# Sixteen modulation columns of an adaLN block: from VectorE reductions to TensorE column groups, with the first loads in another order

## The chip, the cores and the metric

The kernel runs on one core of one Trainium2 chip. The metric is the device time of one execution in microseconds (us). A core has five engines with a queue of instructions each: TensorE (PE in the profile, its weight loads PEld), VectorE (DVE), ScalarE (ACT), GpSimd (POOL) and SyncE (SP), which here issues the DMAs. Each engine works through its own queue in order; semaphores tie the queues together.

## The reference, cut to what matters

```
mod = (silu(c) @ w_mod).reshape(1, 6, 1, 1024)
sa, ca, ga, sb, cb, gb = (mod[:, i] for i in range(6))
h = layernorm(x) * (1 + ca) + sa
x = x + ga * attention(h, wq, wk, wv, wo, beta)
h = layernorm(x) * (1 + cb) + sb
out = x + gb * ((gelu(h @ w_gate) * (h @ w_up)) @ w_down)
```

The input x has 2048 rows of 1024. The attention works on 4 segments of 512 rows with 32 heads of 32, and carries a memory matrix from segment to segment. `c` is one row of 1024 and `w_mod` is 1024 by 6144, so `mod` is one row of 6144 numbers: 48 columns of 128 in the kernel's layout. The first 16 columns are sa (0 to 7) and ca (8 to 15). The very first product of the attention needs them.

## The kernel before, in words

The kernel has three parts: a startup, the attention (32 steps, one for each half of the segments, group of four heads and segment), and the feed-forward, which takes some two thirds of the time.

In the startup, segment 0 of x (four tiles of 128 rows, each in two halves `x0`) is normalised: `norm_seg_stats` takes mean and variance on VectorE (`bn_stats` L233, `bn_aggr` L236, add L238), raises to the power -1/2 on GpSimd (L239), forms the shift on VectorE (`mr`, L244) and scales on ScalarE (L246). `norm_seg` then makes, for each of the 8 slices kt of 128 model columns, four transposes on TensorE (`tpa`, L330), one ScalarE pass that applies the modulation (`h`, L332: column kt of `modT` as the shift, column 8 + kt as the scale), a rounded copy on ScalarE (`hha`, L335) and the remainder on VectorE (`hla`, L336). Products of two fp32 numbers are made of three with such pairs. `first_part` is the first use: for each kt it multiplies `hha` and `hla` with the k, v and q weights of group 0 (12 products of 256 columns at L366, three of 512 at L372), which are themselves split in pairs by `split_w` (L197 on ScalarE, L199 on VectorE).

A modulation column comes from `mod_col` (L188): 128 rows of `w_mod` transposed, 1024 long, are multiplied with `scb` (silu(c), repeated on all 128 partitions) and summed on VectorE; a scale column gets 1.0 added (L193). `scb` is made by `row_of` through two products on TensorE (L162) and two copies on ScalarE (L163). The 16 first columns take 16 loads of 512 KB into 8 buffers (`wm_a` to `wm_d`, two halves each), in the order scale, shift for kt = 0, 1, and so on. The other 32 columns are made the same way, one or two in each later step.

The order of TensorE's and SyncE's instructions in the startup is the program's. On VectorE, ScalarE and GpSimd a planner orders them by the program's order and by when it expects the inputs; only an instruction under `keep_in_program_order` is pinned behind the instruction that the program gave to its engine just before. That holds for the `bn_stats` of segment 1 (`norm_stats`, L229 to L235). The startup's loop (L1432) runs

```
for kt, _ in enumerate(first_part(0, 0, 0)):
    next(nseg, None)
    if kt == 1:
        W[0][2] = split_w(raw0[1], wsp_tile("w0_1"), nc.vector)
    if kt >= 4:
        norm_seg_stats(1, x1h, (kt - 4,))
```

With two turns of `norm_seg` taken ahead of it, the order is: products of kt, transposes of kt + 2, and from kt = 4 on the statistics of one tile of segment 1. Step 0 then opens with the eight turns of `norm_seg(1, ...)`, the transposes of segment 1 (first tile to last), followed by its k and v products. The loads are issued as: c, beta, 8 of x0 (256 KB each), the weights k, v and q of group 0 (512 KB each), 8 columns of `w_mod`, 8 more as buffers come free, and 4 of segment 1 (512 KB each).

Two copies on ScalarE (L1439) fill 32 partitions of the two key tiles `ks` (2048 elements each) with a constant pattern `selj`.

Of the kernel before, what the change touches and what calls it, by code (L numbers as in the profile page):

```python
# [14 lines left out]
ALU = mybir.AluOpType  # L15
# [4 lines left out]
P = 128  # L20
# [13 lines left out]


@with_exitstack
def block_kernel(ctx: ExitStack, tc: tile.TileContext, x, c, wmod, wq, wkv, wo, beta, wg, wu, wd, out):
    nc = tc.nc
    f32 = lambda ap: ap.bitcast(F32)

# [29 lines left out]
    def tmp_tile(name):  # L70
        return big.tile([P, L], F32, name=name, tag="tmp", bufs=4)
# [8 lines left out]
    def s_ps(name):  # L80
        return psum.tile([P, L], F32, name=name, tag="s", bufs=5)
# [4 lines left out]
    def t2(name, tag, bufs=1, dt=F32, shape=(P, L)):  # L86
        return (p1 if tag in ("qs", "row") else pa).tile(list(shape), dt, name=name, tag=tag, bufs=bufs)

    def cs(shape, name, dt=F32, **kw):
        return const.tile(shape, dt, name=name, **kw)  # L90
# [1 line left out]

    ccol = cs([P, KT], "ccol")
    nc.sync.dma_start(ccol, c)
    bb = cs([P, H], "bb")
    nc.sync.dma_start(bb, bass.AP(tensor=beta.tensor, offset=beta.offset, ap=[[0, P], [1, H]]))
    def fetch(src, name):
        r = raw_tile("r" + name)
        nc.sync.dma_start(r, src)
        return r  # L100

    x0 = [[], []]
    for i in range(4):
        for h in range(2):
# [1 line left out]
            t = t2(f"x0_{i}_{h}", tag, bufs=bufs)  # L106
            nc.sync.dma_start(t, x[i * P:(i + 1) * P, h * L:(h + 1) * L])
            x0[h].append(t)
    raw0 = [fetch(wkv[0, 0], "k0"), fetch(wkv[0, 1], "v0"), fetch(wq[0], "q0")]


    ones = cs([P, P], "ones")
# [33 lines left out]
    def sigmoid(dst, src):  # L146
        nc.scalar.activation(dst, src, AF.Exp, scale=-1.0)
        nc.vector.tensor_scalar_add(dst, dst, 1.0)
        nc.vector.reciprocal(dst, dst)
# [16 lines left out]
    def row_of(*a):  # L166
        for _ in row_parts(*a):
            pass
# [1 line left out]
    scol = cs([P, KT], "scol")  # L170
    sigmoid(scol, ccol)
    nc.vector.tensor_mul(scol, scol, ccol)
    scb = t2("scb", "row", shape=(P, D))
    row_of(scb, scol, tmp_tile, "sc")
    gall = cs([P, H], "gall")
    sigmoid(gall, bb)
    omg = pa.tile([P, H], F32, name="omg")
    nc.vector.tensor_scalar(omg, gall, -1.0, 1.0, op0=ALU.mult, op1=ALU.add)
    modT = cs([P, 48], "modT")

    def mod_load(r, w=None):
        if w is None:
            w = raw_tile(f"wm{r}")
        nc.sync.dma_start(w, wmod[r])
        return r, w

    def mod_col(r, w, behind=False):
        i = nc.vector.tensor_tensor_reduce(out=w, in0=w, in1=scb, scale=1.0, scalar=0.0,  # L188
                                           op0=ALU.mult, op1=ALU.add, accum_out=modT[:, r:r + 1])
        if behind:  # L190
            tc.keep_in_program_order(i)
        if r // 8 in (1, 4):
            nc.vector.tensor_scalar_add(modT[:, r:r + 1], modT[:, r:r + 1], 1.0)  # L193
# [256 lines left out]
    def first_part(n, g, s):  # L450

        nm = f"{g}_{s}"
        kn, vx = kv_tiles(n, nm)
        kv = [(mm_ps if t < 2 else s_ps)(f"kv{nm}_{t}") for t in range(4)]
        psq = o_ps("q" + nm)
        for kt in range(KT):
            for t in range(4):
                kv_mm(kv[t][:, :2 * P], g, s, t, kt)
            q_mm(psq, g, s, kt)
            yield  # L460
        for t in range(4):
            kv_out(kv[t][:, :2 * P], kn, vx, t, 1)
        k_out(n, s, nm, kn, vx)
        q_out(n, s, nm, psq)
# [947 lines left out]
    with tc.manual_schedule(engines={mybir.EngineType.PE}):  # L1412
        with tc.manual_schedule(engines={mybir.EngineType.SP}):
            free = [wsp_tile("wm_a"), wsp_tile("wm_b")] + [
                t2(f"wm_{q}", "qs", bufs=2, dt=F32R, shape=(P, 4, L)).rearrange("p (a b) t -> p a (b t)", a=2) for q in "cd"]
            spare = [f32(w[:, h]) for w in free for h in range(2)]
            order = [r for kt in range(KT) for r in (8 + kt, kt)]
            got = [mod_load(r, spare[i]) for i, r in enumerate(order[:8])]
            norm_seg_stats(0, x0)
            W[0] = [None] * 3  # L1420
            for i in (0, 2):
                W[0][(1, 2, 0)[i]] = split_w(raw0[i], wsp_tile(f"w0_{i}"), nc.vector)
            nseg = norm_seg(0, x0)
            for i, r in enumerate(order):
                mod_col(*got[i])
                if i + 8 < len(order):
                    got.append(mod_load(order[i + 8], spare[i % 8]))
                if i in (1, 3):
                    next(nseg)
            x1h = [fetch(x[L + i * P:L + (i + 1) * P, :], f"x1_{i}") for i in range(4)]  # L1430
            x1h = [[t[:, h * L:(h + 1) * L] for t in x1h] for h in range(2)]
            for kt, _ in enumerate(first_part(0, 0, 0)):  # L1432
                next(nseg, None)
                if kt == 1:
                    W[0][2] = split_w(raw0[1], wsp_tile("w0_1"), nc.vector)
                if kt >= 4:
                    norm_seg_stats(1, x1h, (kt - 4,))
        for k in ks_t:
            nc.scalar.activation(k[96:128], selj[96:128].unsqueeze(2).to_broadcast([32, 4, L]), AF.Copy)  # L1439
        norm_a = norm_tiles(x, hT_d, (2, 3), 1, 0, "a")  # L1440
        next(norm_a)
        for n in range(len(steps) + 1):
            work = {k: none for k in "VSAMKQN"}
            if n > 0:
                work["V"] = values(n - 1, *steps[n - 1][1:])
            if n < len(steps):
                work["S"] = scores(n, *steps[n][1:])
                work["A"] = sums(n, *steps[n][1:])
                work["M"] = memory(n, *steps[n][1:])
            work["N"] = norm_seg(1, x1h) if n == 0 else norm_a  # L1450
            side = none
            if n in (14, 15):
                hT[n - 12] = []
                side = load_hT(hT_d, n - 12, hT[n - 12], f"h{n - 12}")
            if n == 30:
                side = load_hT(oT_d, 0, oh[0], "o0")
            if n + 1 < len(steps):
                _, g, s = steps[n + 1]
                work["K"] = kv_part(n + 1, g, s)
                work["Q"] = q_part(n + 1, g, s)  # L1460
            else:
# [81 lines left out]
```

## Time and profile before

| | |
|---|---|
| time, median of 3 runs | 2927.32 us |
| lowest and highest run | 2924.64, 2929.8 us |
| the profiled execution, its own time | 2932.13 us |
| span of its trace | 2930.4 us |
| TensorE busy | 2838.5 us, 97% of the span |
| TensorE busy in the first 73 us (first of 40 slices) | five tenths; 9 tenths in nearly all others |
| VectorE, ScalarE, GpSimd busy | 64%, 43%, 30% |
| granted TensorE clock, mean | 0.992 |

The busy shares are averages over stages with different limits. The span begins with the first instruction of the trace; all times in the rows below count from there.

### The profile page before, as it was taken

What the parts mean: (1) busy time and instruction counts of PE and PEld (TensorE: products, weight loads), DVE (VectorE), ACT (ScalarE), POOL (GpSimd) and SP (SyncE); (2) the same over time, 40 slices, a digit from 0 to 9 for tenths busy, and PEclk for the clock granted to TensorE, in tenths of its full rate; (3) what the DMA queues carried; (4) which work ended last, traced back from release to release, by engine and by line L of the source; (5) the groups of instructions that cost most, each with busy time, mean ns of one, the idle gap of its engine ahead of it and who ended that gap; (6) DMA issues with size and microseconds to landing.
All of it is one profiled execution on the core that took longest, in us unless ns stands there. A gap on an engine that the chain in (4) does not pass through costs nothing.

```text
span 2930.4 us, 48825 instructions
## 1 busy us (share of the span) xinstructions
PE 2838.5 (97%) x17248; PEld 2534.1 (86%) x17248; DVE 1860.8 (64%) x4293; ACT 1265.3 (43%) x3112; POOL 882.6 (30%) x1428
## 2 busy tenths in 40 slices
PE   5999999999999999999999999999999999999998
PEld 4788888888888787899999999899899998999997
DVE  7565667766667724656666666756566675666667
ACT  6677766676767624355433232322122222221221
POOL 0333334433332523544456452112211111111110
PEclk9999999999999999999999999999999999999999
DMA  7567666756464647778798676978877788777775
GB/s 236 114 130 147 143 108 134 147 131 123 98 130 87 170 165 245 272 288 319 271 335 331 270 288 251 377 288 304 313 280 281 284 330 312 283 283 284 283 283 206
DMA packets 236053, 682.97 MB, mean 233 GB/s; under 512 B 23712, under 2 KB 62624, under 8 KB 225312
## 3 DMA queue, kind: packets, MB, share of 16 engines
q1 hardware_dynamic: 235808, 679.85, 71.4%
q8 instruction: 136, 2.23, 0.3%
q14 instruction: 109, 0.89, 0.1%
HBM read 454.32 MB, written 175.11 MB: 215 GB/s over the span
## 4 chain that ended last, share of the span: by engine, by line
PE 76%; DVE 8%; DMA 7%; ACT 4%; issue 3%; POOL 2%; SPq 0%; DVEq 0%; POOLq 0%; ACTq 0%
PE f L1042 32%; PE kv L366 9%; PE d L1285 8%; PE y L627 4%; PE q L372 3%; PE T L557 3%; PE dc L1222 2%; PE ds L1222 2%; PE db L1222 2%; PE da L1222 2%; PE S L493 2%; PE O L566 2%; ACT sj L497 2%; DVE qs L510 1%; PE dd L1222 1%
## 5 line engine op out<-in xcount | busy, mean ns | idle before, releaser
L1042 PE MATMUL f<-A,B 128*128 128x320 f32 (+1 forms) x7056 | 1120.9, 319 | 19.1 <-DVE c L1060 7.3
L1042 PEld LDWEIGHTS f<-A,B 128*128 128x128 f32 x7056 | 1105.7, 189 | 29.8 <-DVE c L1060 8.3
L495 DVE CUSTOM_DVE_ANT_0 sj<-S,mask 128x384 f32<-128x384 f32 (+3 forms) x512 | 229.7, 487 | 226.2 <-PE S L493 207.7
L497 ACT ACTIVATE sj<-sj,mm 128x384 f32<-128x384 f32 (+3 forms) x512 | 281.7, 553 | 113.7 <-DVE mm L495 113.4
L790 POOL TENSOR_TENSOR rt<-rt 128x256 f32<-128x256 f32 x104 | 76.9, 761 | 767.9 <-DMA rt<-wd 679.8
L560 POOL TENSOR_SCALAR_AFFINE_SELECT pt<-pt 128x128 f32<-128x128 f32 x512 | 171.4, 356 | 338.2 <-ACT pt L559 332.6
L1285 PE MATMUL d<-wd,hc 128*128 128x512 f32 x1128 | 259.9, 390 | 0.9 <-DVE hc L1105 0.7
L1285 PEld LDWEIGHTS d<-wd,hc 128*128 128x128 f32 x1128 | 211.1, 188 | 44.9 <-DVE hc L1105 1.0
L366 PE MATMUL kv<-w,hha 128*128 128x256 f32 x1024 | 206.8, 288 | 3.4 <-ACT hha L335 3.4
L366 PE MATMUL kv<-w,hhh 128*128 128x256 f32 x1024 | 201.7, 285 | 0.0
L559 ACT ACTIVATE pt<-T 128x256 f32<-128x256 f32 (+3 forms) x512 | 181.8, 456 | 38.7 <-PE T L557 34.6
L202 POOL TENSOR_TENSOR w<-r,w 128x256 fp32r<-128x256 f32 x180 | 133.5, 773 | 165.7 <-ACT w L197 165.6
L366 PEld LDWEIGHTS kv<-w,hha 128*128 128x128 f32 x1024 | 169.2, 194 | 4.9 <-ACT hha L335 4.3
L1114 ACT ACTIVATE hc<-g 128x256 fp32r<-128x256 f32 (+2 forms) x182 | 78.4, 444 | 212.9 <-DVE acc L1231 126.9
L1065 ACT ACTIVATE g<-g 128x320 f32<-128x320 f32 (+1 forms) x84 | 41.2, 490 | 298.6 <-DVE g L1064 298.6
L366 PEld LDWEIGHTS kv<-w,hhh 128*128 128x128 f32 x1024 | 166.4, 192 | 0.3 <-issue 0.2
L1309 DVE TENSOR_TENSOR acc<-acc,d 128x512 f32<-128x512 f32 x176 | 119.1, 685 | 61.2 <-PE d L1285 59.8
L557 PEld LDWEIGHTS T<-qs,ks 128*128 128x128 f32 x512 | 81.2, 190 | 84.8 <-issue 35.1
L366 PE MATMUL kv<-w,hla 128*128 128x256 f32 x512 | 147.1, 287 | 6.6 <-DVE hla L336 5.9
L557 PE MATMUL T<-qs,ks 128*128 128x256 f32 (+2 forms) x512 | 128.5, 360 | 20.1 <-DVE qs L510 7.5
L366 PE MATMUL kv<-w,hlh 128*128 128x256 f32 x512 | 145.1, 283 | 0.0
L1052 ACT ACTIVATE c<-f 128x320 f32<-128x320 f32 (+1 forms) x84 | 38.2, 455 | 233.9 <-PE f L1042 233.7
(246 smaller groups left out, 5257.1 us busy)
## 6 DMA issues: line engine op xcount, KB each, us to landing
B<-bc_d SPq DMA_DIRECT2D x392, 512.0 KB, 6.9
bc_d<-B SPq DMA_DIRECT2D x196, 512.0 KB, 6.8
wd<-wc_d SPq DMA_DIRECT2D x54, 1024.0 KB, 8.3
wc_d<-wd SPq DMA_DIRECT2D x28, 1024.0 KB, 8.0
rt<-wd SPq DMA_DIRECT2D x54, 512.0 KB, 8.1
ks<-kh SPq DMA_DIRECT2D x64, 256.0 KB, 5.6
qs<-qh SPq DMA_DIRECT2D x64, 256.0 KB, 7.5
wm<-wmod SPq DMA_DIRECT2D x32, 512.0 KB, 5.5
```

Source lines behind the costliest of these rows:

```text
L202: eng.tensor_sub(w[:, 1, k:k + 256], r[:, k:k + 256], f32(w[:, 0, k:k + 256]))
L366: nc.tensor.matmul(ps, b[:, sl], w[:, a], start=(kt == 0 and a == 0 and b is hi), stop=(kt == KT - 1 and a == 1), **kw)
L495: nc.vector.tensor_tensor_reduce(out=sj[:, :nv], in0=ps[:, :nv], in1=mask[:, L - nv:], scale=-1.0, scalar=3.4e38, op0=ALU.add, op1=ALU.min ...
L497: nc.scalar.activation(sj[:, :nv], sj[:, :nv], AF.Exp, bias=mm[:, j, i:i + 1], scale=-1.0, accum_out=ll[:, i, j:j + 1])
L557: nc.tensor.matmul(ps[:, :nn], ks[:, j, kc * P:(kc + 1) * P], qs[:, j, L - nn:], start=True, stop=True)
L559: nc.scalar.activation(pt, ps[:, nn - n:nn], AF.Exp)
L560: nc.gpsimd.affine_select(pt[:, :P], pt[:, :P], pattern=[[1, P]], compare_op=ALU.is_ge, fill=0.0, base=0, channel_multiplier=-1)
L627: nc.tensor.matmul(ps, b[:, i * P:(i + 1) * P], w[:, a, g % 2], start=(g == 0 and a == 0 and b is hi), stop=(g == G - 1 and a == 1))
L1042: nc.tensor.matmul(ps, B[m, i][:, a, kt * P:(kt + 1) * P], A[p, i, kt][b], start=(start and kt == 0 and a == 0 and b == 0), stop=(kt == 3 ...
L1222: nc.tensor.matmul(ps, t[:, c:c + P], B(a), start=(start and a == 0 and b == 0), stop=(stop and a == 1), skip_group_check=True)
L1285: nc.tensor.matmul(ps, hid[m][:, b, tt * P:(tt + 1) * P], down_w[m][:, a, nb * L:(nb + 1) * L], start=(m == chunks[0] and a == 0 and b == ...
L1309: nc.vector.tensor_add(dst, dst, ps)
```

## The change

The 16 first columns are no longer VectorE sums. `w_mod`'s first 2048 columns are laid out on the host as 16 blocks of 512 KB (`wm0`), four for each of four groups b of two kt. `first_mods(b, w)` multiplies on TensorE: silu(c), one value for each partition and k, repeated 32 times (`scr`, 128 x 32 for each k) is the stationary side, 128 columns of weights are the moving side, and the four products of one k go to four column groups of 32 in one PSUM tile. That is 32 fp32 products for a group. ScalarE copies the tile to SBUF (`modr`), a transpose turns it, and two VectorE instructions write the two shift and the two scale columns of `modT`.

`scb` (still needed for the other 32 columns) and beta's sigmoid are made behind the first products. Beta and the v and q weights are loaded later: the order is c, x0, k, group 0, q, group 1, v, group 2 (as its buffers come free), group 3, beta, segment 1. The two `ks` copies go from ScalarE to GpSimd. TensorE's startup order becomes a written list, in which `a` to `d` are the four groups (two turns each: products and copy, then transpose; `a` takes one turn at each of its two places), `n` a turn of `norm_seg`, `f` the products of the next kt (the ninth `f` is the tail of `first_part`), and `s` the statistics of one tile of segment 1.

```diff
-    bb = cs([P, H], "bb")
-    nc.sync.dma_start(bb, bass.AP(tensor=beta.tensor, ...))
...
-    raw0 = [fetch(wkv[0, 0], "k0"), fetch(wkv[0, 1], "v0"), fetch(wq[0], "q0")]
+    raw0 = [fetch(wkv[0, 0], "k0")]
...
-    scb = t2("scb", "row", shape=(P, D))
-    row_of(scb, scol, tmp_tile, "sc")
+    scr = tmp_tile("scr")[:, :32 * KT].rearrange("p (k i) -> p k i", i=32)
+    nc.vector.tensor_copy(scr, scol.unsqueeze(2).to_broadcast([P, KT, 32]))
...
+    def first_mods(b, w):
+        ps = s_ps(f"mod{b}")[:, :P]
+        for k in range(KT):
+            for j in range(4):
+                nc.tensor.matmul(ps[32 * j:32 * j + 32], scr[:, k], w[k // 2][:, (k % 2 * 4 + j) * P:(k % 2 * 4 + j + 1) * P],
+                                 start=(k == 0), stop=(k == KT - 1), skip_group_check=True)
+        row = tmp_tile(f"modr{b}")[:, :P]
+        nc.scalar.activation(row, ps, AF.Copy)
+        yield
+        pt = s_ps(f"modt{b}")[:, :P]
+        nc.tensor.transpose(pt, row, ident)
+        pv = pt.rearrange("p (j i) -> p j i", i=32)[:, :, 0]
+        nc.vector.tensor_copy(modT[:, 2 * b:2 * b + 2], pv[:, :2])
+        nc.vector.tensor_scalar_add(modT[:, 8 + 2 * b:10 + 2 * b], pv[:, 2:], 1.0)
...
-            order = [r for kt in range(KT) for r in (8 + kt, kt)]
-            got = [mod_load(r, spare[i]) for i, r in enumerate(order[:8])]
+            mods = [mods_load(0)]
+            raw0.append(fetch(wq[0], "q0"))
+            mods.append(mods_load(1))
+            raw0.insert(1, fetch(wkv[0, 1], "v0"))
...
-            for i, r in enumerate(order):
-                mod_col(*got[i])
-                if i + 8 < len(order):
-                    got.append(mod_load(order[i + 8], spare[i % 8]))
...
+            for i, q in enumerate("a a n n f b f n n f c f n n f d f n n s f s f s s f".split()):
...
+            sigmoid(gall, bb)
+            nc.vector.tensor_scalar(omg, gall, -1.0, 1.0, op0=ALU.mult, op1=ALU.add)
+            scb = t2("scb", "row", shape=(P, D))
+            row_of(scb, scol, tmp_tile, "sc")
         for k in ks_t:
-            nc.scalar.activation(k[96:128], selj[96:128].unsqueeze(2).to_broadcast([32, 4, L]), AF.Copy)
+            nc.gpsimd.tensor_copy(k[96:128], selj[96:128].unsqueeze(2).to_broadcast([32, 4, L]))
```

## Rows read from the trace of the kernel before

**Rows 1.** Busy time of each engine in two stretches.
```profile
0.00:62.00 62.00, 33.62 (x167) 26.45 (x168) 46.81 (x121) 34.94 (x50) 6.30 (x19) 0.93 0.68 241
62.00:100.00 38.00, 33.80 (x216) 30.52 (x215) 25.11 (x67) 27.78 (x65) 11.14 (x18) 0.93 0.65 140
```
**Rows 2.** VectorE's groups of instructions between 15 and 45 us.
```profile
L188 DVE CUSTOM_DVE_ANT_0 wm_b<-wm_b,scb 128x1024 f32<-128x1024 f32 x4 | 4.9, 1218 | 0.0
...
L336 DVE TENSOR_TENSOR hla<-h,hha 128x512 fp32r<-128x512 f32 x6 | 4.1, 688 | 0.0
```
**Rows 3.** TensorE in order of time: start, duration, instruction, idle before it.
```profile
10.36 3.78 PE L162 MATMUL sc<-scdg,ones 128*128 128x512 f32 x4 [10.36 <-DVE scdg L156]
...
23.34 0.58 PE L366 MATMUL kv<-w,hha 128*128 128x256 f32 x1 [3.40 <-ACT hha L335]
...
28.21 1.05 PE L330 MATMUL tpa<-ident,x 128*128 128x128 f32 x4
...
42.06 0.39 PE L366 MATMUL kv<-w,hla 128*128 128x256 f32 x1 [2.80 <-DVE hla L336]
...
48.29 0.60 PE L330 MATMUL tpa<-ident,x 128*128 128x128 f32 x4
48.65 0.36 PE L366 MATMUL kv<-w,hha 128*128 128x256 f32 x1
...
50.85 0.28 PE L366 MATMUL kv<-w,hha 128*128 128x256 f32 x1
...
61.12 4.71 PE L330 MATMUL tpa<-ident,rx 128*128 128x128 f32 x29 [2.58 <-ACT rx L246]
```
**Rows 4.** VectorE in order of time.
```profile
16.20 1.23 DVE L188 CUSTOM_DVE_ANT_0 wm_a<-wm_a,scb 128x1024 f32<-128x1024 f32 x1 [0.58 <-DMA wm_a<-wmod]
...
47.97 1.28 DVE L233 BATCH_NORM_STATS2 sta<-rx 128x6 f32<-128x512 f32 x2
...
50.57 0.68 DVE L336 TENSOR_TENSOR hla<-h,hha 128x512 fp32r<-128x512 f32 x1
51.17 1.28 DVE L233 BATCH_NORM_STATS2 sta<-rx 128x6 f32<-128x512 f32 x2
...
60.01 0.21 DVE L244 TENSOR_SCALAR mr<-mva,rsa 128x1 f32<-128x1 f32 x1
63.82 0.69 DVE L336 TENSOR_TENSOR hla<-h,hha 128x512 fp32r<-128x512 f32 x1 [3.60 <-ACT hha L335]
65.00 0.69 DVE L336 TENSOR_TENSOR hla<-h,hha 128x512 fp32r<-128x512 f32 x1 [0.50 <-ACT hha L335]
```
**Rows 5.** Two stretches of ten us; the last column is DMA in GB/s.
```profile
0.00:10.00 10.00, 0.00 (x0) 0.00 (x0) 4.88 (x18) 1.72 (x3) 2.09 (x12) 1.00 0.66 208
10.00:20.00 10.00, 6.27 (x12) 2.59 (x12) 7.44 (x30) 9.35 (x12) 1.66 (x3) 1.00 1.03 416
```
**Rows 6.** ScalarE in order of time.
```profile
10.62 1.90 ACT L1439 ACTIVATE ks<-selj 32x2048 fp32r<-32x2048 f32 x1 [5.29 <-DVE selj L135]
...
15.64 3.63 ACT L246 ACTIVATE x<-x,mr,rsa 128x512 f32<-128x512 f32 x5
...
20.11 1.05 ACT L197 ACTIVATE w<-rq 128x1024 fp32r<-128x1024 f32 x1
21.06 0.77 ACT L332 ACTIVATE h<-tpa,modT 128x512 f32<-128x512 f32 x1
```
**Rows 7.** TensorE products in column groups of 32 (L566, attention), in order of time.
```profile
101.90 1.07 PE L566 MATMUL O<-pt,vx 128*32 128x512 f32 x8
...
111.69 0.86 PE L566 MATMUL O<-pt,vx 128*32 128x256 f32 x16
```
**Rows 8.** A group of GpSimd instructions, then GpSimd in order of time.
```profile
L225 POOL TENSOR_TENSOR hlo<-ro,hho 128x512 fp32r<-128x512 f32 x16 | 23.5, 1479 | 29.6 <-ACT hho L222 25.7 <-PE y L627 3.1 <-issue 0.4
...
85.62 2.88 POOL L202 TENSOR_TENSOR w<-r,w 128x256 fp32r<-128x256 f32 x4 [1.51 <-ACT w L197]
```
**Rows 9.** VectorE in order of time: one instruction at two places.
```profile
87.88 0.65 DVE L504 TENSOR_TENSOR mt<-mm,mt 128x16 fp32r<-128x16 f32 x1
...
123.15 0.18 DVE L504 TENSOR_TENSOR mt<-mm,mt 128x16 fp32r<-128x16 f32 x1
```

More of the change, by code (lines that the diff above doesn't have):

```diff
@@ L36, in block_kernel @@
 @with_exitstack
-def block_kernel(ctx: ExitStack, tc: tile.TileContext, x, c, wmod, wq, wkv, wo, beta, wg, wu, wd, out):
+def block_kernel(ctx: ExitStack, tc: tile.TileContext, x, c, wm0, wmod, wq, wkv, wo, beta, wg, wu, wd, out):
     nc = tc.nc
@@ L94, in block_kernel @@
     nc.sync.dma_start(ccol, c)
-    bb = cs([P, H], "bb")
-    nc.sync.dma_start(bb, bass.AP(tensor=beta.tensor, offset=beta.offset, ap=[[0, P], [1, H]]))
     def fetch(src, name):
@@ L172, in block_kernel @@
     nc.vector.tensor_mul(scol, scol, ccol)
-    scb = t2("scb", "row", shape=(P, D))
-    row_of(scb, scol, tmp_tile, "sc")
+    scr = tmp_tile("scr")[:, :32 * KT].rearrange("p (k i) -> p k i", i=32)
+    nc.vector.tensor_copy(scr, scol.unsqueeze(2).to_broadcast([P, KT, 32]))
     gall = cs([P, H], "gall")
-    sigmoid(gall, bb)
     omg = pa.tile([P, H], F32, name="omg")
-    nc.vector.tensor_scalar(omg, gall, -1.0, 1.0, op0=ALU.mult, op1=ALU.add)
     modT = cs([P, 48], "modT")
+    def first_mods(b, w):
[12 more added lines that the diff above has]
+        nc.vector.tensor_scalar_add(modT[:, 8 + 2 * b:10 + 2 * b], pv[:, 2:], 1.0)
     def mod_load(r, w=None):
@@ L183, in mod_load @@
             w = raw_tile(f"wm{r}")
-        nc.sync.dma_start(w, wmod[r])
+        nc.sync.dma_start(w, wmod[r - 16])
         return r, w
@@ L1416, in block_kernel, with mods_load @@
             spare = [f32(w[:, h]) for w in free for h in range(2)]
-            order = [r for kt in range(KT) for r in (8 + kt, kt)]
-            got = [mod_load(r, spare[i]) for i, r in enumerate(order[:8])]
+            def mods_load(b):
+                w = spare[b % 2 * 4:b % 2 * 4 + 4]
+                for q in range(4):
+                    nc.sync.dma_start(w[q], wm0[4 * b + q])
+                return first_mods(b, w)
+            mods = [mods_load(0)]
+            raw0.append(fetch(wq[0], "q0"))
+            mods.append(mods_load(1))
+            raw0.insert(1, fetch(wkv[0, 1], "v0"))
             norm_seg_stats(0, x0)
@@ L1423, in block_kernel @@
             nseg = norm_seg(0, x0)
-            for i, r in enumerate(order):
-                mod_col(*got[i])
-                if i + 8 < len(order):
-                    got.append(mod_load(order[i + 8], spare[i % 8]))
-                if i in (1, 3):
-                    next(nseg)
[L1430 to L1434, printed above, removed]
-                    W[0][2] = split_w(raw0[1], wsp_tile("w0_1"), nc.vector)
-                if kt >= 4:
-                    norm_seg_stats(1, x1h, (kt - 4,))
+            first = first_part(0, 0, 0)
+            x1h, tile1 = None, 0
+            for i, q in enumerate("a a n n f b f n n f c f n n f d f n n s f s f s s f".split()):
+                if q == "n":
+                    next(nseg)
+                elif q == "f":
+                    next(first, None)
+                elif q == "s":
+                    norm_seg_stats(1, x1h, (tile1,))
+                    tile1 += 1
+                else:
+                    for _ in range(1 if q == "a" else 2):
+                        next(mods["abcd".index(q)], None)
+                if i == 1:
+                    mods.append(mods_load(2))
+                if i == 5:
+                    W[0][2] = split_w(raw0[1], wsp_tile("w0_1"), nc.vector)
+                    mods.append(mods_load(3))
+                    bb = cs([P, H], "bb")
+                    nc.sync.dma_start(bb, bass.AP(tensor=beta.tensor, offset=beta.offset, ap=[[0, P], [1, H]]))
+                    x1h = [fetch(x[L + i * P:L + (i + 1) * P, :], f"x1_{i}") for i in range(4)]
+                    x1h = [[t[:, h * L:(h + 1) * L] for t in x1h] for h in range(2)]
+            sigmoid(gall, bb)
+            nc.vector.tensor_scalar(omg, gall, -1.0, 1.0, op0=ALU.mult, op1=ALU.add)
+            scb = t2("scb", "row", shape=(P, D))
+            row_of(scb, scol, tmp_tile, "sc")
         for k in ks_t:
-            nc.scalar.activation(k[96:128], selj[96:128].unsqueeze(2).to_broadcast([32, 4, L]), AF.Copy)
+            nc.gpsimd.tensor_copy(k[96:128], selj[96:128].unsqueeze(2).to_broadcast([32, 4, L]))
         norm_a = norm_tiles(x, hT_d, (2, 3), 1, 0, "a")
@@ L1525 @@
         "c": np.asarray(c).reshape(KT, P).T,
-        "wmod": np.asarray(w_mod).T.reshape(48, P, D),
+        "wm0": np.asarray(w_mod)[:, :2 * D].reshape(4, 2, P, 2, 4, 2, P).transpose(4, 0, 2, 1, 3, 5, 6).reshape(16, P, D),
+        "wmod": np.asarray(w_mod)[:, 2 * D:].T.reshape(32, P, D),
         "wq": cols(np.ascontiguousarray(by_head(A_wq)).reshape(D, D), P),
```

## The prediction

> **What bounds the kernel now.** I read the page first. TensorE is busy 97% of the span, and only the first of its 40 slices shows five tenths. So I cut the span into stretches [rows 1]: up to 62 us TensorE works 33.6 us and stands idle 28.4; in the next 38 us it loses 4.2. The change touches only that first stretch; what it gains or loses there moves the rest as a whole, since the attention's order is fixed and its inputs start from the same place. The most that can be won is a part of 28 us, 1% of the time.
>
> Then the groups of instructions, for what fills the stretch. The modulation sums are 16 of 1.22 us on VectorE, 19.5 us in all [rows 2]; the reader should see that VectorE has no idle time between them. TensorE in order of time shows where this hurts [rows 3]: at 42.06 the products of kt 4 have waited 2.80 us for `hla`, a VectorE subtraction of 0.69 us queued among sums. But it shows too that VectorE's sums are not what ends the stretch: they are over at about 43 us, and TensorE waits again at 61.12 for ScalarE, which has scaled segment 1's last tile. I followed that chain back [rows 4]: statistics of tile 0 at 47.97 right behind one `hla`, of tile 1 at 51.17 right behind the next, the last tile's `mr` at 60.01. Each tile's `bn_stats` is pinned behind the previous tile's `mr`, and that waits for GpSimd's power; so the four tiles form a ladder with one rung per tile: 47.97 to 50.57 is 2.6 us, and from 51.17 to 60.22 three rungs take 3.0 us each. Everything of step 0 waits for the ladder's end. The question is when the ladder can start after the change.
>
> **What goes.** The 19.5 us of sums on VectorE, the two products for `scb` on TensorE (3.78 us at 10.36 [rows 3], moved behind the products), and two `ks` copies of 1.90 us on ScalarE [rows 6]. None of these engines is what the new order waits for (below), so of this relief only the gap of 2.80 us and the start count.
>
> **When the first products start.** DMA moves 208 GB/s in the first ten us and 416 in the next [rows 5]; 512 KB at 416 GB/s take 1.26 us. The first `w_mod` buffer is there at 16.20 [rows 4], with two weights ahead of it that now come later: 16.2 - 2.5 = 13.7 us for the first quarter of group 0, 17.5 for the last. Two of eight k remain then, with copy, transpose and two short VectorE instructions: about 19.5. Meanwhile x0 is scaled (until 19.27 before [rows 6], earlier without the `ks` copy in front). The q weight lands at 18.8 and its ScalarE split (1.05 us) goes first. Before, from the start of `h` at 21.06 [rows 6] to the first product at 23.34 [rows 3] it took 2.3 us with a weight split between. I put the first `f` at 22.0, against 23.34 [rows 3]. Bounds: 20.5 if `h` goes ahead of the split and the clock is up, 28 in the second rival.
>
> **The cost of a column group.** No row has exactly this, but the attention's products in column groups are near: four products of 512 columns (8 instructions) last 1.07 us; those of 256 and 128 together, 384 columns, 0.86 [rows 7]. That is 0.21 us per 128 columns and 0.2 fixed. A group here has 8 rounds of 128 columns: 8 x 0.21 + 0.2 = 1.9 us. Bounds: twice that, 3.8, at half pace, and 1.7 without the fixed part. The transpose behind it must wait for ScalarE's copy in the same queue: some 0.7 us for the copy, two handovers and the transpose. Each of groups b, c and d thus takes 2.6 us out of TensorE's order, 7.8 in all, and before they took nothing of it.
>
> **The order of TensorE, step by step.** At full pace one `f` is 2.2 us (48.65 to 50.85) and one `n` 0.36 (48.29 to 48.65); the first `f` ran at half pace, 4.9 us from 23.34 to 28.21 [rows 3]. In the new list an `f` stands directly behind two `n` whose output it needs. From the transposes at 48.29 [rows 3] to their `hla` at 50.57 [rows 4] are 2.3 us, and `hha` is there 0.15 before; so that `f` starts 2.1 us after the first `n`, having waited 1.4, and loses 0.55 more on the first `hla`. Before, two transposes of distance covered this.
>
> - f0: 22.0, 3.2 us (between full and half pace): 25.2
> - b: 27.8; f1: 30.0
> - n n, f2: starts 32.1, ends 34.9
> - c: 37.5; f3: 39.7
> - n n, f4: starts 41.8, ends 44.6
> - d: 47.2; f5: 49.4
> - n n: transposes at 49.4, `hla` of kt 6 from 51.6, that of kt 7 a rung of 1.2 later (63.82 to 65.00 [rows 4]), done at 53.5.
>
> The loads don't bind: at 1.26 us for 512 KB, group 1 is there at 23.8, group 2 at 30.1, group 3 at 35.2 and segment 1 at about 40, each ahead of its use here. SyncE's queue waits at groups 2 and 3 for buffers that groups 0 and 1 free at 18 and 27; behind it wait beta and segment 1, needed later still.
>
> **The ladder.** The first `s` now stands behind both last `n`, where it stood between them; its `bn_stats` is pinned behind `hla` of kt 7. It starts at 53.5 and has four rungs, of 2.6 to 3.0 us: 10.4 to 12.1, of which I take the middle, 11.2, since the tail's VectorE work still interleaves: 64.7, against 60.22. That is +4.5 us. The row products of `scb`, which now stand between the tail and segment 1's transposes, lie in TensorE's wait for the ladder (2.58 us idle at 61.12 alone [rows 3]); without that cover they cost up to their 3.78.
>
> **Sum.** Between 28.21 and 48.29 TensorE had 5 `f` and 5 `n` to do, 12.8 us, in 20.1: it lost 7.3 to waits and half pace. The new list loses two waits with their `hla` in the same part, 3.9 us. So f5 ends at -1.3 (first `f` earlier) - 1.7 (shorter) + 7.8 (groups) + 3.9 - 7.3, less 0.3 for a transpose that now stands behind it: +1.1, 49.4 against 48.3. The ladder starts 5.5 later than before (53.5 against 47.97), because both `n` now stand between, and is 1.0 shorter (11.2 against 12.25, which held an `hla` of 0.6): +4.5 us. On the profiled execution's 2932.13 us (its span 2930.4) that makes 2936.6. That execution lies 4.8 over the median of 2927.32, so for the median it is 2932, +0.15%. This kernel's measurement tells about 0.2%, 5.9 us, from no change: most likely no difference that can be told, on the slow side.
>
> **Rivals.**
>
> *VectorE's relief counts in full (faster).* The column groups (5.7 us), their tails and the two waits (2.1 and 3.9) all fit into TensorE's 28.4 us of idle time [rows 1]: +4.5 - 11.7 = -7.2, 2920. For it speak that idle time and a VectorE that is full from 20 to 43 us. Against it: the list puts the groups between products, where TensorE is not idle, and ScalarE's 2.1 us behind each pair of transposes stays. It decides if the `hla` of kt 7 ends before 43. Chance 0.07.
>
> *It evens out.* First `f` at 20.5 and all at full clock: group b then ends at 25.0, when its load does, 2.8 ahead of the list, and rungs of 2.6 give 0.8 more: +0.9 us, 2928. Chance 0.13.
>
> *The `ks` copies hold up the powers (slower).* GpSimd gets two copies of 2048 elements a partition. Nearest rows: 512 elements with two inputs take 1.48 us [rows 8], so 5.9 for 2048; ScalarE's 1.90 is the lower bound. Their input `selj` is ready near 10.6, when the first ScalarE copy had waited for it [rows 6], just as the statistics of x0 come in; the planner put the ScalarE copy there in front of the scaling. If both stand ahead of the powers of tiles 1 to 3, these come at 10.5 + 11.8 = 22.3, scaling ends near 25.5 and f0 starts at 27.6: +5.6 on the list, 2938. If one does, the powers come at 16.4 and scaling ends near 20, about when `modT` is there: nothing. A copy also meets VectorE: L504, two SBUF inputs, takes 0.65 us at 87.88 beside GpSimd's subtraction and 0.18 at 123.15 without [rows 8, 9]. It decides if f0 starts later than 25. Chance 0.18.
>
> The Trainium skill, SBUF — State Buffer, section Who interferes with whom, states the rule behind the last rows: a VectorE instruction with two SBUF inputs is shut out for the whole of a GpSimd instruction that reads SBUF. By that rule, which these rows agree with in kind, one long copy would hold a VectorE subtraction of the startup up to the copy's whole length, where four short ones hold it for one at most; the rival's time would then hold even with the copies behind the powers, if they meet the first `hla` or the weight split.
>
> **How the numbers follow.** The list's case has 0.62. Its own range is +0.5 to +8.5: the rungs' bounds of 0.8 each way, b, c and d with tails of 0.4 to 1.0, one group at half pace (+1.9), the row products uncovered (+2 of 3.78). About a quarter of it lies above 5.9 us. Slower by over 0.2%: 0.18 + 0.18 = 0.36; faster: 0.07; the rest, 0.57, within. The predicted time is the list's, 2932. The range 2926 to 2940 takes in the evened-out case and the slow rival, and leaves out the fast one and the ends.
>
> **What would show it.** Right: no L188 in the first 45 us; four bursts of 128*32 products of about 2 us, each followed by some 0.7 us of idle time at a transpose; waits of TensorE for `hha` ahead of the third, fifth and seventh kt; segment 1's first `bn_stats` directly behind the eighth `hla`, near 53; the 29 transposes of 61.12 near 65.5. Wrong: powers (L239) of x0 behind GpSimd copies, or a first product after 25; groups at half pace throughout (+1.9 each); or a start that ends as computed while the sum differs, which would put the cause behind 100 us, where the planner may order VectorE, ScalarE and GpSimd anew.

## The result, and the profile after

| | before | after |
|---|---|---|
| median | 2926.97 us (16 runs, 2920.44 to 2937.09) | 2942.15 us (16 runs, 2935.59 to 2948.95) |
| ratio to before | | 1.0049 [1.004, 1.0059] |
| the profiled execution, its own time | 2932.13 us | 2937.35 us |
| span of its trace | 2930.4 us | 2935.6 us |

The change makes the kernel slower by 0.49%, some 14 us, where +4.5 was forecast; 2942 lies outside the range of 2926 to 2940. The interval says 11.7 to 17.3 us. The two profiled executions differ by only 5.2: before's lies 5 over its median and after's 5 under. So I set the traces side by side at the same instruction of TensorE: the attention's first product `S` starts at 76.33 before and at 88.06 after, +11.7; from 106 us of after on the same instructions are 12.9 apart, through the attention. The other 1.2 us are the q products behind that, which run partly at half pace in after: the granted clock is 0.75 of full speed from 100.5 to 106 us there and 1.00 from 88.8 to 94 before (a mean of stretches at 1.2 and 2.4 GHz). The wait ahead of them is in both; before, then after:
```profile
88.68 0.44 PE L390 MATMUL kT<-ident,kn 128*128 128x128 f32 x2 [2.75 <-ACT kn L383]
```
```profile
100.22 0.69 PE L403 MATMUL kT<-ident,kn 128*128 128x128 f32 x2 [2.56 <-ACT kn L396]
```
12.9 of 2927 is 0.44%, within the interval. It is only in the feed-forward, where both kernels do the same work, that this pair of executions comes together: 5.3 us apart at 2000 us, 5.1 at the end. The loss is made in the startup.

The page's first lines of after, then two stretches, the first cut 0.9 us behind the start of segment 1's transposes, as in [rows 1]:
```profile
PE 2845.0 (97%) x17508; PEld 2535.5 (86%) x17508; DVE 1848.5 (63%) x4262; ACT 1260.2 (43%) x3114; POOL 886.4 (30%) x1430
```
```profile
0.00:73.50 73.50, 42.24 (x429) 32.10 (x430) 32.98 (x90) 31.07 (x52) 9.99 (x21) 0.95 0.61 208
73.50:111.50 38.00, 33.45 (x204) 29.35 (x203) 24.04 (x65) 26.74 (x62) 10.04 (x15) 0.91 0.55 128
```
VectorE works 33.0 us in a stretch of 73.5 where it worked 46.8 in 62. TensorE has 8.6 us more to do, most of it the groups, and does not do it in its idle time: that was 28.4 us and is 31.3. The second stretch is as before (4.55 idle, 4.2 before). So nearly the whole loss is a startup 11.5 us longer.

TensorE of after in order of time, answering [rows 3]:
```profile
13.09 2.27 PE L183 MATMUL mod<-wm_a,scr 128*32 128x128 f32 x32 [13.09 <-DMA wm_a<-wm]
...
16.82 1.08 PE L183 MATMUL mod<-wm_b,scr 128*32 128x128 f32 x16 [0.19 <-DMA wm_b<-wm]
...
20.19 0.45 PE L189 MATMUL modt<-ident,modr 128*128 128x128 f32 x1 [2.29 <-ACT modr L186]
...
23.73 0.58 PE L379 MATMUL kv<-w,hha 128*128 128x256 f32 x1 [1.39 <-ACT hha L348]
...
28.32 1.08 PE L183 MATMUL mod<-wm_c,scr 128*32 128x128 f32 x32
...
30.67 0.33 PE L189 MATMUL modt<-ident,modr 128*128 128x128 f32 x1 [0.40 <-ACT modr L186]
30.76 0.36 PE L379 MATMUL kv<-w,hha 128*128 128x256 f32 x1
...
32.96 1.03 PE L343 MATMUL tpa<-ident,x 128*128 128x128 f32 x8
35.67 0.38 PE L379 MATMUL kv<-w,hha 128*128 128x256 f32 x1 [1.67 <-ACT hha L348]
36.39 0.38 PE L379 MATMUL kv<-w,hla 128*128 128x256 f32 x1 [0.34 <-DVE hla L349]
...
53.52 1.03 PE L343 MATMUL tpa<-ident,x 128*128 128x128 f32 x8
...
68.34 2.04 PE L160 MATMUL sc<-scdg,ones 128*128 128x512 f32 x2 [5.85 <-DVE scdg L154]
70.79 1.97 PE L160 MATMUL sc<-scdg,ones 128*128 128x512 f32 x2 [0.41 <-DVE scdg L154]
72.60 2.57 PE L343 MATMUL tpa<-ident,rx 128*128 128x128 f32 x22
```
The loads come as forecast: group a's first quarter is multiplied at 13.09 (forecast 13.7), the last at 16.82, and no later wait here is for a DMA. Between 28.32 and 53.52 the list runs at full pace with the same numbers each time: group 2.44, `f` (the products of the next kt; f0 to f7 are those of kt 0 to 7) 2.2, then 2.71 from the start of a pair of transposes to the next `f`, of which 1.67 is idle, and that `f` 2.93 with 0.34 of waiting for `hla`. At the end stand two products for `scb`, after 5.85 us of idle time, and only then segment 1's transposes.

The other engines around the first `f`; GpSimd, VectorE, then ScalarE:
```profile
10.17 1.90 POOL L1472 CAST ks<-selj 32x2048 fp32r<-32x2048 f32 x1 [0.41 <-DVE seli L135]
...
14.24 1.89 POOL L1472 CAST ks<-selj 32x2048 fp32r<-32x2048 f32 x1
...
16.59 0.55 POOL L252 TENSOR_TENSOR rsa<-rsa,mhalf 128x1 f32<-128x1 f32 x1 [0.47 <-DVE rsa L251]
```
```profile
10.22 1.99 DVE L172 COPY scr<-scol 128x256 f32<-128x256 f32 x1
...
14.34 1.80 DVE L139 TENSOR_TENSOR seli<-seli,eye 128x4 f32<-128x4 f32 x1
```
```profile
17.43 1.52 ACT L259 ACTIVATE x<-x,mr,rsa 128x512 f32<-128x512 f32 x2 [0.64 <-DVE mr L257]
18.85 1.04 ACT L210 ACTIVATE w<-rk 128x1024 fp32r<-128x1024 f32 x1
19.80 0.25 ACT L186 ACTIVATE modr<-mod 128x128 f32<-128x128 f32 x1
```
A `ks` copy takes 1.90 us on GpSimd, the forecast's lower bound. An instruction of VectorE that starts 0.05 or 0.1 us behind one ends with it or 0.14 later: 1.99 us for `scr`, 1.80 for an addition of four numbers a partition. x0's last power comes at 16.59, the last scaling ends at 18.95, and `modr` goes at 19.80, behind a weight split, though its products ended at 17.9.

VectorE at the ladder:
```profile
56.20 1.29 DVE L349 TENSOR_TENSOR hla<-h,hha 128x512 fp32r<-128x512 f32 x2 [4.38 <-ACT hha L348]
57.41 1.28 DVE L246 BATCH_NORM_STATS2 sta<-rx 128x6 f32<-128x512 f32 x2
...
67.51 0.68 DVE L154 TENSOR_TENSOR scdg<-ident,scol 128x512 f32<-128x512 f32 x1
68.63 0.21 DVE L257 TENSOR_SCALAR mr<-mva,rsa 128x1 f32<-128x1 f32 x1 [0.44 <-POOL rsa L252]
...
69.96 0.68 DVE L154 TENSOR_TENSOR scdg<-ident,scol 128x512 f32<-128x512 f32 x1
```
The eighth `hla`, the second of the two at 56.20, starts 6.2 us later than in [rows 4] (56.81), and the first statistics directly behind it. The products of `scb` need `scdg`, which VectorE makes at 67.51 and 69.96, around the last `mr`: the row does not stand under the ladder, it stands behind it.

### The profile page after: what moved, and what is told of

It is laid out like the page before. It is cut to its first block, busy times and chain, and to the rows that moved or that the text cites. A ratio compares the mean times of both kernels' runs of the same rounds, so it can differ in the third digit from the quotient of the medians.

```text
span 2935.6 us, 49333 instructions
## 1 busy us (share of the span) xinstructions
PE 2845.0 (97%) x17508; PEld 2535.5 (86%) x17508; DVE 1848.5 (63%) x4262; ACT 1260.2 (43%) x3114; POOL 886.4 (30%) x1430
## 4 chain that ended last, share of the span: by engine, by line
PE 76%; DVE 7%; DMA 6%; ACT 3%; issue 3%; POOL 2%; SPq 0%; DVEq 0%; POOLq 0%; ACTq 0%
PE f L1055 32%; PE kv L379 9%; PE d L1298 8%; PE y L640 4%; PE q L385 3%; PE T L570 3%; PE dc L1235 2%; PE ds L1235 2%; PE S L506 2%; PE db L1235 2%; PE da L1235 2%; PE O L579 2%; PE dd L1235 1%; DVE qs L523 1%; ACT sj L510 1%
```

## The experiments

"First S" is the start of the attention's first product in the profiled execution (before 76.33, after 88.06); it leaves out what single executions add later. In the nine versions that were timed several times, after among them, the distance from before in time and the one in first S agree within 2.6 us (d1: 12.6 and 11.5 us; d4: 8.8 and 7.0; c3: -4.7 and -3.3), so first S tells most of what a change is worth. "Half pace" means that products take about twice as long as elsewhere; where a granted clock stands beside it, it is the share of full speed in that stretch. The "row products" are the two products that make `scb`. Where no ratio stands, the time is a single run (before beside it: 2924.5 for the first four, 2926.07 for e5 to e7 and c1).

**The groups' own price.** e3 makes group a alone; the columns of the others are copies of its columns.
```diff
 def first_mods(b, w):
+    if b > 0:
+        nc.vector.tensor_copy(modT[:, 2 * b:2 * b + 2], modT[:, :2])
+        nc.vector.tensor_copy(modT[:, 8 + 2 * b:10 + 2 * b], modT[:, 8:10])
+        yield
+        return
```


> The changed kernel without the products, copy and transpose of groups b, c and d; their columns of modT are copies of group a's (the result is not the reference's). Theory (TensorE's list is the bound): each group stood in the list for 2.43 us (28.32 to 30.76, 38.60 to 41.03, 48.87 to 51.31), so f5 ends at 46.2 instead of 53.52 and the first scores product comes 7.3 earlier, at 80.8. Rival (the groups only fill time in which TensorE would wait for ScalarE's h and hha): less than 3 of the 7.3 come back, first scores above 85.

2934.51 us; first S 81.13, 6.9 earlier. Three groups of 2.43 stand in TensorE's order at nearly full price; nothing hides them. Without them first S is still 4.8 us behind before's.

**Turns one products-length ahead.** e4, again as d3:
```diff
-"a a n n f b f n n f c f n n f d f n n s f s f s s f"
+"a a n n f b n n f f c n n f f d n n f s f s f s s f"
```


> The changed kernel with another list, a a n n f b n n f f c n n f f d n n f s f s f s s f: each pair of transposes one f earlier, directly behind its group. Theory (the f behind a pair of n waits for ScalarE and VectorE): the waits of 1.67 and 0.34 ahead of the third, fifth and seventh kt (2.0 each) shrink to 0.5 or less, and the eighth hla no longer waits for f5, so the ladder starts 2 x 1.6 + 2.2 = 5 us earlier, at 52.3 instead of 57.4, and the first scores product comes at 83. Rival (VectorE or ScalarE is behind already, and the wait only moves to the f after): first scores at 87 to 88.

> The changed kernel with each pair of transposes one f earlier, once more and timed. Theory (waits of the list): first scores at 82 to 84.5, and a ratio 0.0017 under the changed kernel's, 1.003. Rival (pace): first scores above 86, ratio as the changed kernel's.

e4: 2935.54 us, first S 83.09, 5.0 earlier, though its first `f` came 1.3 later (25.01). d3, 11 runs: 2934.33 us, ratio 1.0026 [1.0014, 1.0037], first S 81.38. TensorE of d3:
```profile
30.75 1.04 PE L343 MATMUL tpa<-ident,x 128*128 128x128 f32 x8
...
34.19 0.39 PE L379 MATMUL kv<-w,hla 128*128 128x256 f32 x1 [0.16 <-DVE hla L349]
```
Of 1.67 us of idle time behind a pair, and 0.34 for `hla` behind that, 0.16 is left; the eighth `hla` starts at 50.35, 6.2 earlier than in d1 (below): two waits of 2.0, and one `f` of 2.2 that now stands behind the last pair.

**Only the statistics forward.** e5:
```diff
-"a a n n f b f n n f c f n n f d f n n s f s f s s f"
+"a a n n f b f n n f c f s n n f s d f s n n s f f f"
```


> The changed kernel with only the four s moved forward in its list: a a n n f b f n n f c f s n n f s d f s n n s f f f. Theory (segment 1's ladder, pinned behind the eighth hla, is what the startup ends with): VectorE is idle for 3.7 to 4.4 us between the bursts of hla, and segment 1's loads are issued at 31.5 to 34.2; the four rungs then lie beside TensorE's products, the last mr is done before 61 instead of 68.84, and the run of segment 1's transposes waits only for the tail and the row products: it starts 5 to 9 us earlier, first scores product at 79 to 83 instead of 88.06. Rival (VectorE, ScalarE or the loads of segment 1 are late too, so rungs in front of hla delay the products of segment 0 by what they save): first scores above 86.

2942.69 us; the ladder starts at 42.94 instead of 57.41, the last `mr` ends at 63.55 instead of 68.85, and first S is at 88.96. TensorE of e5 shows where the wait went:
```profile
59.68 0.38 PE L379 MATMUL kv<-w,hha 128*128 128x256 f32 x1 [3.29 <-ACT hha L348]
...
70.63 1.89 PE L160 MATMUL sc<-scdg,ones 128*128 128x512 f32 x2 [1.64 <-DVE scdg L154]
72.32 4.63 PE L343 MATMUL tpa<-ident,rx 128*128 128x128 f32 x32
```
The transposes of segment 1 stay at 72.3, for another reason than in after. There TensorE is done with the products in front of the row products at 62.5 and the ladder ends at 68.85. In e5 the ladder ends earlier, but TensorE gets through its list 5.0 us later: 1.0 is a longer wait for group d's `modr` and 1.6 one for the last `hha`, both behind a scaling of segment 1 on ScalarE, and 2.2 is half pace (group b takes 3.01 us instead of 2.44, f6 4.36 instead of 2.83). Behind that, TensorE waits for `scdg` on VectorE as before.

**The row products.** e1 gives them to step 0 behind segment 1's first transposes; e8 later still, with the `ks` copies behind (below); d4 is e8 with `scdg` pinned to its place in VectorE's program order.
```diff
-            row_of(scb, scol, tmp_tile, "sc")
+            sc_row = row_parts(scb, scol, tmp_tile, "sc")
+            todo += [(at, lambda: next(sc_row, None)) for at in (10, 13, 16)]  # e8, d4: (19, 22, 25)
...
-            nc.vector.tensor_tensor(dg..., op=ALU.mult)
+            i = nc.vector.tensor_tensor(dg..., op=ALU.mult)
+            if name == "sc":                                                   # d4
+                tc.keep_in_program_order(i)
```


> The changed kernel with one edit: the row products of scb (L160) leave their place between the tail of first_part and segment 1's transposes and come in step 0, behind its eight N turns. Theory (uncovered row products): in the changed kernel the last mr is done at 68.84 and segment 1's run of transposes starts at 72.60, where 0.9 would do as before (60.22 to 61.12); so 2.9 us come back, the run starts near 69.7 and the first scores product, at 88.06 there, near 85.2. Rival (the products lie in the ladder's shadow, as the prediction had it): 88 stays, within 0.5.

> The changed kernel with two edits: GpSimd's copies behind x0's powers (alone they brought the first scores product from 88.06 to 83.61) and the row products of scb late in step 0, behind its scores, where they meet none of segment 1's hla. Theory (both are terms of their own): from the last mr to the first scores product 16.1 us as before the change, not 19.0 to 19.2; the first scores product at 80.7, and the median some 7 us under the changed kernel's, 4 to 6 over the kernel before (ratio 1.0015 to 1.002). Rival (the 2.9 are lost to half pace in the stretch, not to the row products): 18 or more from mr to scores.

> As e8 (GpSimd's copies behind the powers, row products late in step 0), with the two VectorE instructions that feed the row products pinned behind the work of step 0, so that they no longer stand among segment 1's hla, where they delayed the last one by 1.2 us. Theory: from the last mr to the first scores product 16.1 to 16.8 us, not 18.0; first scores at 81.5 to 84, ratio 1.002. Rival (the stretch is long because TensorE is at half pace there): 18 again.

e1: 2940.09 us, first S 89.59; e8: 2939.57, ratio 1.0046 [1.0032, 1.006], 87.62; d4: 2935.97, ratio 1.003 [1.0021, 1.004], 83.29. The startups of e1 and e8 were slower on the way to the ladder, so I take the time from the end of the last `mr` to first S, into which the pace up to there does not enter, though the pace within it does: 16.1 us before, 19.2 after, 18.0 in e1, 17.9 in e8, 16.3 in d4. Of the 3.1 that after loses here, 2.85 lie ahead of segment 1's transposes, and these come back in all three: from the end of the last `mr` to the transposes it is 3.76 us in after, 0.91 in e1, e8 and d4 and 0.90 before. Of e1, VectorE, then TensorE:
```profile
71.40 0.21 DVE L257 TENSOR_SCALAR mr<-mva,rsa 128x1 f32<-128x1 f32 x1 [0.15 <-POOL rsa L252]
```
```profile
72.52 4.78 PE L343 MATMUL tpa<-ident,rx 128*128 128x128 f32 x29 [2.74 <-ACT rx L259]
```
In e1 and e8 another 1.7 to 1.8 us go behind the transposes. The planner puts `scdg` between segment 1's `hla` there, which delays the last `hla` by 0.6, as VectorE of e8 shows:
```profile
78.75 0.69 DVE L154 TENSOR_TENSOR scdg<-ident,scol 128x512 f32<-128x512 f32 x1
...
81.01 0.68 DVE L154 TENSOR_TENSOR scdg<-ident,scol 128x512 f32<-128x512 f32 x1
```
The other 1.1 are half pace from the last `hla` to first S: 5.3 us at a granted clock of 0.55 in e8, 4.3 at 0.73 in d4, 4.1 at 0.77 before. Whether the late `hla` bring that about isn't shown; e2, e5 and e7 have a long slow stretch there without `scdg` between the `hla`. Moved and pinned, the row costs 0.2. First S of d4 is 3.1 us ahead of d2's (86.37).

**The `ks` copies.** e2 gives them back to ScalarE; e6, again as d2, leaves them on GpSimd behind x0's powers; d1 is after once more, beside d2 to d4.
```diff
-            nc.gpsimd.tensor_copy(k[96:128], selj...)
+            nc.scalar.activation(k[96:128], selj..., AF.Copy)                      # e2
...
             norm_seg_stats(0, x0)
+            for k in ks_t:                                                         # e6, d2
+                tc.keep_in_program_order(nc.gpsimd.tensor_copy(k[96:128], selj...))
```


> The changed kernel with the two ks copies back on ScalarE. Theory (GpSimd's copies hold up VectorE and the last power): the copy of scr on VectorE takes 0.3 instead of 1.99 us, the seli addition 0.15 instead of 1.80, x0 is scaled near 17.3 instead of 18.95, modr no longer waits behind a weight split, and the first f starts at 22.3 instead of 23.73; everything behind it comes 1.4 to 1.9 earlier, the first scores product near 86.4. Rival (ScalarE pays what GpSimd saved, since 1.9 us stand in front of the scaling again): first f at 23.3 to 24, first scores near 88.

> The changed kernel with its two GpSimd copies pinned behind the fourth power of x0. Theory (a copy of 1.9 us on GpSimd shuts VectorE out, and the second holds the last power): scr is copied in 0.3 instead of 1.99 us, x0 is scaled near 17.3 instead of 18.95, and the first f starts 1 to 1.6 us earlier than 23.73 (if the copies do not meet VectorE's weight split at 19.9 to 22.4, in which case 0 to 0.5). Rival (what sets the first f is modr behind a weight split on ScalarE, whatever x0 does): first f at 23.4 or later.

> The changed kernel itself, once more. If the startup's loss is a matter of the list and the queues, the first f starts at 23.5 to 24.5, the first scores product at 87 to 90, and the ratio is 1.004 to 1.006. If it is a matter of TensorE's pace, the first scores product differs by more than 3 us from 88.06.

> The changed kernel with GpSimd's copies pinned behind x0's powers, once more and timed. Theory (the copies cost 1.5 us at the first f, and the first profile had 2 to 3 more from TensorE being at full pace already in the first f): first f at 21 to 22.6, first scores at 84 to 87, ratio 1.002 to 1.004. Rival (the copies cost the whole 4.4): first scores at 83.6 again and a ratio of 1.002 or less.

e2: 2945.31 us, first `f` at 25.84. ScalarE of e2:
```profile
19.01 1.90 ACT L1472 ACTIVATE ks<-selj 32x2048 fp32r<-32x2048 f32 x1
...
21.90 0.26 ACT L186 ACTIVATE modr<-mod 128x128 f32<-128x128 f32 x1
```
`scr` takes 0.29 us on VectorE there, but the second copy stands in front of `modr`, 2.1 us later than in after. e6: 2932.95 us, first `f` at 21.14, first S 83.61, 4.4 earlier. The repeat with d1 beside it corrects that: d1 2939.16, ratio 1.0043 [1.0028, 1.0059], first S 87.81; d2 2938.89, ratio 1.0038 [1.0024, 1.0051], first `f` 22.13, first S 86.37. VectorE and ScalarE of d2:
```profile
10.41 0.29 DVE L172 COPY scr<-scol 128x256 f32<-128x256 f32 x1
```
```profile
18.16 0.28 ACT L186 ACTIVATE modr<-mod 128x128 f32<-128x128 f32 x1 [0.54 <-PE mod L183]
```
The copies ahead of the powers cost about 1.4 us at the first product; the times of d1 and d2 can't tell that apart. The rest of e6's 4.4 was pace: its f0 took 2.93 us, those of after and d2 4.6 and 4.5.

**The order of the loads.** e7 loads v and q with k, ahead of group 0.
```diff
-    raw0 = [fetch(wkv[0, 0], "k0")]
+    raw0 = [fetch(wkv[0, 0], "k0"), fetch(wkv[0, 1], "v0"), fetch(wq[0], "q0")]
...
-            raw0.append(fetch(wq[0], "q0"))
...
-            raw0.insert(1, fetch(wkv[0, 1], "v0"))
```


> The changed kernel with the loads of the v and q weights back ahead of group 0. Theory (the order of need brings group 0 earlier by two loads of 1.26 us, but modr then waits on ScalarE): group 0's products end near 20.4 instead of 17.9, modr follows at once, and the first f starts at 24 to 25 instead of 23.73, a loss of 1 at most. Rival (the first f hangs on group 0's landing): 2.5 later, at 26.2, and all behind it too.

2948.74 us, first `f` at 26.25, 2.5 later, first S 92.0. The new order of the loads is worth its two transfers.

**Before, with another ladder.** b1 is the kernel before, with each tile of segment 1 scaled one tile later, so that the next tile's `bn_stats` need not wait for the power (the added lines are put in words).
```diff
             mv, rs = norm_stats([halves[0][i], halves[1][i]], f"a{s}_{i}", s > 0)
-            norm_scale([halves[h][i] for h in range(2)], mv, rs, f"{s}_{i}")
+            # segment 1: the shift and the scaling of tile i - 1 here, the last two at the end
```


> The kernel before the change, with one edit: the scaling of a tile of segment 1 (mr and ScalarE) is given one tile later, so that the next tile's bn_stats is pinned behind the sum of the tile before and no longer behind its mr and GpSimd's power. Theory (the ladder ends the startup before the change too): a rung falls from 3.0 to about 1.9 us, the last mr comes 3 to 4 us earlier than 60.22, the first scores product at 72.5 to 73.5 instead of 76.33, and the time falls by 3 us (ratio 0.999). Rival (the ladder waits with other work that ends as late): scores at 76, ratio 1.

2927.46 us, ratio 0.9997 [0.9989, 1.0006]: no difference, though the last `mr` ends 3.8 and first S stands 2.7 earlier. By 96 us 1.2 are left, from 145 us on it is 0.2 behind. Pace takes it back, in two stretches: 1.5 us by 91 us, with a granted clock of 0.83 in 80 to 90 us where before shows 1.00, and 1.5 between 136 and 142 us, with 0.93 in 120 to 145 us where before shows 1.00. Why the clock was lower in these stretches isn't known.

**All together.** c1 has d3's idea with the statistics further forward, copies behind, the row late and `modr` on VectorE; c2 another list with the same, without `modr`; c3 is c2 with b1's ladder.
```diff
+"a a n n f b n n f f c n n f s f d n n s f s f s f f"   # c1
+"a a n n f b n n f f c n n f s f s d s n n s f f f f"   # c2, c3
```


> All together: list a a n n f b n n f f c n n f s f d n n s f s f s f f (transposes one f earlier, statistics of segment 1 between), GpSimd's copies pinned behind x0's powers, the row products of scb in the second half of step 0, modr copied by VectorE. By the list theory: no f waits for more than 0.5, the groups' 7.3 us remain, the ladder is hidden: from the first f at 22.5, eight f at 2.2 with 2.4 more at half pace, three groups at 2.4, six n at 0.35, waits 1.5: 53; tail and segment 1's transposes follow, first scores 16 later, at 69 to 72, ahead of the kernel before (76.33). By the rival (what the startup loses is VectorE's, ScalarE's and GpSimd's time, not the order): above 78.

> The changed kernel with the list a a n n f b n n f f c n n f s f s d s n n s f f f f, GpSimd's copies behind x0's powers and the row products late in step 0 (modr stays on ScalarE). Theory: first f at 21.2, seventh kt without waits, ladder over near 54, segment 1's transposes at 55 to 56, first scores at 71.5 to 73; 4 us ahead of the kernel before: ratio 0.9985. Rival (what is won in the startup is given back behind it): scores at 72 and a ratio of 1 or more.

> As the run before it in this list, with the scaling of segment 1's tiles one tile later as well. Theory (TensorE's list is then the bound, the ladder is not): the same first scores product within 1 us, 71 to 72.5, and the same ratio, 0.9985. Rival (the last rung still sets segment 1's transposes): 1.5 to 3 us earlier.

c1: 2923.51 us, first S 76.98. c2: 2926.81, ratio 0.9997 [0.9988, 1.0006], 76.6. c3: 2923.24, ratio 0.9984 [0.9975, 0.9993], 73.0; one of its 11 runs showed 6979.96 us, is not in the ratio, and nothing here explains it. The first stretch of c3, and TensorE at the end of it:
```profile
0.00:73.50 73.50, 52.79 (x501) 42.82 (x502) 35.64 (x98) 39.62 (x66) 9.66 (x21) 0.95 0.73 232
```
```profile
54.86 0.49 PE L352 MATMUL tpa<-ident,rx 128*128 128x128 f32 x3
55.70 1.64 PE L352 MATMUL tpa<-ident,rx 128*128 128x128 f32 x13 [0.35 <-ACT rx L259]
...
73.00 0.64 PE L515 MATMUL S<-ks,qs 96*128 96x256 f32 x4
```
TensorE does 10.6 us more in the same 73.5 us than in after, and segment 1's transposes start 17.7 earlier. Of the 3.3 us won at first S against before, 1.5 stay from 145 us on; again there is half pace between (granted clock 0.74 from 82 to 95 us). c3 is the only version shown to beat both kernels, by an amount at the edge of what can be told.

## Why the prediction was wrong

The place was right: the startup, with TensorE's written order and the ladder as what sets its end, and the rest moved as a whole. The sum was +4.5 and is +11.5 at segment 1's transposes (61.12 to 72.60). By its own steps:

| step | forecast | measured | more |
|---|---|---|---|
| first `f` starts | 22.0 | 23.73 | +1.7 |
| f0 lasts | 3.2 | 4.6 | +1.4 |
| groups b, c, d | 2.6 each | 2.44, 2.43, 2.43 | -0.5 |
| two waits, from a pair's start to the next `f` | 2.1 each | 2.71 each | +1.2 |
| f2, f4 | 2.8 each | 2.93 each | +0.3 |
| last pair to the eighth `hla` done | 4.1 | 3.9 | -0.2 |
| the ladder | 11.2 | 11.4 | +0.2 |
| last `mr` to segment 1's transposes | 0.9 | 3.8 | +2.9 |

The column "more" makes 7.0, the whole difference.

**The step that failed** is the cover given to the row products: that they "lie in TensorE's wait for the ladder". The 5.85 us of idle time that should cover them were there, but their input `scdg` is made on VectorE, and the planner put one half into the ladder's last rung and the other behind it. The prediction named the price of lost cover, "up to their 3.78"; 2.9 was paid. I had looked for the cover on the engine where the products stand, and not on the one that makes their input. e1, e8 and d4 show it: without the row products in that place, the 3.76 us from the last `mr` to the transposes are 0.91 again. With a fixed place on VectorE as well, 0.2 of the cost is left at first S (d4). That an early `scdg` would have had the products covered where they stood is argued; no run makes it early and leaves them there.

**First `f`, +3.1 with its pace.** The loads were right. 1.4 of it are the `ks` copies (d2 against d1, and `scr`'s 0.29 against 1.99). The slow rival had the mechanism, VectorE shut out and powers held up, but priced a copy at 5.9 us from rows with two inputs; at 1.90 the copies cost 1.4, and `f0` starts at 23.73, below the 25 from which that rival was to decide. The Trainium skill, SBUF — State Buffer, section Who interferes with whom, states that a blocked instruction waits for the whole of the other and isn't merely slowed; the 1.99 and 1.80 us beside copies of 1.90 and 1.89 agree. f0 I had put between full and half pace; it ran at half pace. The lengths of its products show that, one `q` product of f0 and one of f1:
```profile
27.40 0.63 PE L385 MATMUL q<-hla,w 128*128 128x512 f32 x1
...
32.50 0.40 PE L385 MATMUL q<-hla,w 128*128 128x512 f32 x1
```
The view's granted clock does not: it reads 1.00 for f0 in after (23.73 to 28.32) too.

**The waits, +1.5 with their `f`.** I took the delay from one transpose to its `hla` where one slice was on its way. In the new list two slices come together, and ScalarE makes both `h` (1.45 us) ahead of the first `hha`:
```profile
33.65 1.45 ACT L345 ACTIVATE h<-tpa,modT 128x512 f32<-128x512 f32 x2 [3.03 <-PE tpa L343]
34.99 1.15 ACT L348 ACTIVATE hha<-h 128x512 fp32r<-128x512 f32 x2
```
d3 shows that the waits belong to the pair: with an `f` between, they go. That it is ScalarE's order of the two `h` that makes them longer than 2.1 is read from the trace alone.

**What held.** The price of a group (from the attention's column-group rows), the ladder's length, that it is pinned behind the eighth `hla`, and that VectorE's 19.5 us brought nothing while it stands there. The rival in which the groups fit into idle time fails as argued: e3 gets back 6.9 of 7.3. The sum's errors were nearly all of one sign, and the range had not let them fall together: it went up to +8.5 for the list.

**What stays open** is TensorE's pace. Executions of the same startup differ: f0 took 2.93 us in e6 and 4.5 in d2, the same kernel; in e8 groups b and c start 12.5 us apart, in after 10.3. A window of after, then the same of e8:
```profile
30.00:40.00 10.00, 7.59 (x103) 6.30 (x96) 1.52 (x4) 2.76 (x5) 0.00 (x0) 1.00 0.84 322
```
```profile
30.00:40.00 10.00, 7.60 (x51) 6.52 (x55) 1.52 (x4) 2.76 (x5) 0.00 (x0) 0.83 0.89 332
```
The granted clock is 1.00 and 0.83, and after's stretch holds 1.4 us of group c (from 38.60), e8's 0.3 (from 39.71). No run says what decides it. Three pairs of profiles of one kernel differ at first S by 0.3 (after and d1), 1.7 (e4 and d3) and 2.8 us (e6 and d2), so a single profile of this startup is good to some 3 us, no better.

## What to carry to other kernels

Work taken from an engine that ends earlier than the chain brought nothing here, and put into the order of the engine that the chain runs through it cost nearly its full price; so ask first which queue the end stands in. Work moved under a wait is covered only if every engine that feeds it can do its part there too: follow its inputs back to their queues, and pin them where a planner may put them elsewhere. Where a producer serves several slices, keep one consumer's length between a pair and its use, which took 1.8 us from each wait here.

## What the runs showed of the hardware

- A VectorE copy of 128x256 from SBUF to SBUF took 1.99 us beside a GpSimd copy and 0.29 without; an addition of 128x4 took 1.80 beside one and 0.15 without. A GpSimd copy of 32x2048 took 1.90 us, as long as on ScalarE; the 1.48 us of a GpSimd subtraction of 128x512 [rows 8] is no measure for it.
- A group's 32 fp32 products are 64 instructions in the trace, and 32 of them take 0.90 us at full pace (28.32 to 29.22 in after), 1.8 us for a group; in e8 the first 32 of group b took 1.71 us, counted the same way (27.16 to 28.87).
